# Input loads, one-hot moves and the gate's weights issued at other places of an attention and mixture-of-experts kernel

## The chip, the core and the metric

The kernel runs on one core of a Trainium2 chip. The metric is the device time of one execution in microseconds (us). Lower is better. The core has a matrix engine (PE, with its weight loads shown as PEld), two elementwise engines (DVE and ACT), a third, slower elementwise engine (POOL), and a queue engine (SP) that issues nearly all data transfers of this kernel, one after the other in program order. Each engine works through its own list of instructions in order. A transfer is done by the core's 16 DMA engines after SP has issued it.

## The reference

Three stages follow each other. The first is attention in which a query sees only the keys of its own hash bucket; the second is a dense mixture of eight experts with balanced gates; the third gives each token to one expert.

```python
# attention: q, k, v are (2, 8, 768, 64), proj is (64, 6)
q_bits = (einsum('bhsd,dk->bhsk', q, proj) > 0)      # and k_bits alike
mask = q_bucket[:, :, :, None] == k_bucket[:, :, None, :]
scores = where(mask, scale * q @ k.T, -1e9)
attn = exp(scores - max); attn = attn / (sum(attn) + 1e-9)
x = attn @ v                                         # then (1536, 512)
# experts, dense: w_gate (512, 8), w1 (8, 512, 1024), w2 (8, 1024, 512)
P = exp(x @ w_gate - max)
for _ in range(8): P /= P.sum(1) ; P /= P.sum(0) ; P *= N / E
x = sum over e of P[:, e] * (relu(x @ w1[e]) @ w2[e])
# experts, one per token: greedy by sorted logits, at most N / E tokens each
out[mask_e] = relu(x[mask_e] @ w1b[e]) @ w2b[e]
```

## The kernel before, in words

**Attention.** The 16 heads are taken as eight pairs (`n` = 0 to 7). A pair has two heads of 768 queries, so twelve tiles of 128 queries (`TU = 12`); the text calls the tiles of a pair r0 to r11. One pass of the loop `for t in range(NT + ...)` (L400) writes the instructions of tile `t` and of older tiles that are at later steps. The order is fixed by hand: `PLANS` (L25) lists, for even and odd tiles, which step comes when and how many tiles it lags, and a manual schedule keeps that order on every engine. The steps are:

- `qk` (L277): four PE products into the scores `S`. The operands are the stacked tiles `qa`, `ka`, `qb`, `kb`: rows 0 to 63 hold q or k in a high and a low part, rows 64 to 127 of `qb` and `kb` hold one-hot codes of the bits, so that the mask falls out of the same products.
- `soft`, `expo`, `inv`, `norm`: the maximum on DVE (L284), the exponential on ACT (L289), the reciprocal on DVE (L296), and the multiplication on POOL (L301), three tiles behind.
- `tr` (L309): PE transposes the normalised tile `e`, four to six tiles behind; ACT and DVE split it into two parts (L317, L321); `av` (L331) multiplies with v.
- `xa` and `xp`: after the second head's `av`, ACT copies the sums out (L351) to tiles called `x`, `idle` and `pz` in turn, SP moves them to the other half of the partitions (L352, L353: `xm`, `xc`), and POOL adds and splits them into `X`, the input of the experts (L363 to L365). This happens in tiles r2 to r8 of the next pair: the three pairs of transfers are `xm<-x`, `xm<-idle`, `xm<-pz`, each with its `xc`.
- `pp`, `pa`, `pd` in tiles r0 to r9: the next pair is prepared. PE transposes its q in r0 and r1 and its k in r2 and r3 (L170), ACT and DVE split them (L177 to L182), the bits follow in r4 and r5 (L199), the one-hot tiles `hot0` and `hot1` in r6 to r9 (L222, L230). Finished parts are put on a list, `MOVES`, and SP issues what was on the list at a tile's start at that tile's end (`move`, L159): six moves for q, six for k, two for each `hot`.
- `pv` (`ahead_v`, L372): POOL splits v (L254, L257), and `load(n + 2)` fetches q, k and v of the pair after the next with six transfers (L82).

The tiles `rq`, `rk`, `rv` have two buffers each, so the load of pair n + 2 waits until those of pair n have been read. For pair 0 the last read of `rv` is the step of `PREP_V` at tile 8.

```python
PREP_V = (3, 3, 6, 8)
...
        if r == TU - 1 and n + 2 < NP:
            load(n + 2)
...
        due = len(MOVES)
        for nm, lag, *part in PLANS[t % 2]:
...
        if due:
            move(due)
```

**Experts.** Behind the loop the order is a scheduler's. The weights come in 512 KB pieces through three `raw` buffers and are split into a high part (ACT, L431) and a low part (DVE, L432) in `big`. The gate's products (24 matmuls, L480 and L481, with the weights `wgs` that DVE makes from `wgr`, L466 to L469) give the gate `P`; eight rounds of balancing on DVE, with one small PE product each (L509), run beside the hidden products of the first expert (L567), which is followed by its output products (L586).

Of the kernel before, what the change touches and what calls it, by code (L numbers as in the profile page):

```python
# [9 lines left out]
F32 = mybir.dt.float32  # L10
F32R = mybir.dt.float32r
# [4 lines left out]
OP = mybir.AluOpType  # L16
# [22 lines left out]
def rd(x):  # L39
    return x.bitcast(F32)  # L40
# [3 lines left out]
def kernel(ctx, tc, q, k, v, proj, wg1, w1, w2, wg2, w1b, w2b, out):  # L44
    nc = tc.nc
# [3 lines left out]
    E = wg1.shape[1]  # L49
    F = w1.shape[2]  # L50
    R = S // 128
    NP = B * H // 2
    HP = H // 2
# [4 lines left out]
    consts = ctx.enter_context(tc.tile_pool(name="consts", bufs=1))  # L58
# [10 lines left out]
    ap = actx.enter_context(tc.tile_pool(name="attn", bufs=1))  # L69
# [4 lines left out]
    def load(n, what="qkv"):  # L74
        b, hp = divmod(n, HP)
        for nm, src in (("q", q), ("k", k), ("v", v)):
            if nm in what:
                t = ap.tile([128, R, 2, D], F32, name="r" + nm, bufs=2)
                rows = (slice(0, R // 2), slice(R // 2, R)) if n == 0 and nm != "v" else (slice(0, R),)
                for rs in rows:  # L80
                    for s in range(2):
                        nc.sync.dma_start(t[:, rs, s, :], src[b, 2 * hp + s].rearrange("(p r) d -> p r d", r=R)[:, rs])  # L82
                RAW["r" + nm, n] = t
# [13 lines left out]
    nc.gpsimd.memset(zero, 0.0)  # L97
    pid = ap.tile([128, NB], I32, name="pid")
    nc.gpsimd.iota(pid, pattern=[[0, NB]], base=0, channel_multiplier=1)
    pj = ap.tile([128, 256], F32, name="pj")  # L100
    nc.gpsimd.memset(pj, 0.0)
    pz = ap.tile([128, 256], F32, name="pz")
    nc.gpsimd.memset(pz, 0.0)
# [41 lines left out]
    def stack(n, s, moves):  # L145

        if n == 0 and s == 1 and HELD is not None:
            HELD.append((n, s, moves))
            return
        MOVES.extend((dst[at:at + 64, s], src[64 * s:64 * s + 64]) for dst, at, src in moves)  # L150
        if n == 0:
            move()
# [3 lines left out]
    def move(n=None):  # L156

        for dst, src in MOVES[:n]:
            nc.sync.dma_start(rd(dst), rd(src))  # L159
        del MOVES[:n]  # L160
# [46 lines left out]
    def hot_rows(dst, t, w, s, on_dve=False):  # L207

        rows = slice(64 * s, 64 * s + 64)
        if on_dve:  # L210
            nc.vector.tensor_scalar(dst, t[rows], 0.5 * NB if w else 0.5 * (NB - 2), 1.0 if w else BIG,
                                    op0=OP.is_ge if w else OP.is_gt, op1=OP.subtract if w else OP.mult)
        else:
            nc.scalar.activation(dst, t[rows], AF.Sign if w else AF.Relu, bias=cb[rows, w:w + 1], scale=1.0 if w else BIG)

    def prep_hot(n, w, ch, part):
        c0, c1 = PC[ch]
        if part == 0:
            if ch == 0 and n:
                PREP["o", w, n] = ap.tile([128, S], F32R, name=f"hot{w}", bufs=1)  # L220
            t = (Sp[1] if n == 0 and w == ch == 1 else aps.tile([128, 512], F32, name="tp", bufs=3))[:, :c1 - c0]
            nc.tensor.matmul(t, pat[:, w], PREP["b", n][:, c0:c1], start=True, stop=True)  # L222
            PREP["t"] = t
        if part == 1 and n == 0:
            for s in range(2):
                hots0[s].append((ST[0][2 + w][64:128, s, c0:c1], PREP["t"], w, s))
            hot_rows(*hots0[0].pop(), on_dve=w != ch)
        elif part == 1:
            hot = PREP["o", w, n]
            nc.scalar.activation(hot[:, c0:c1], PREP["t"], AF.Sign if w else AF.Relu, bias=cb[:, w:w + 1],  # L230
                                 scale=1.0 if w else BIG)
            if ch == 1:
                dst = ST[n % 2][2 + w]
                for s in range(2):
                    stack(n, s, ((dst, 64, hot),))

    def prep(n, i, part):
        if i < 4:
            prep_t(n, "qk"[i // 2], i % 2, part)
        elif i < 6:  # L240
            prep_bits(n, i - 4, part)
        else:
            prep_hot(n, (i - 6) // 2, i % 2, part)
# [3 lines left out]
    def prep_v(n, i):  # L247
        x = RAW["rv", n]
        if i == 0:
            VS[n] = ap.tile([128, R, 2, 2, D], F32R, name="vv", bufs=2)  # L250
        vv = VS[n]
        s = i // 2
        if i % 2 == 0:
            nc.gpsimd.tensor_tensor(vv[:, :, s, 0, :], x[:, :, s, :],  # L254
                                    zero[:, :, None].to_broadcast([128, R, D]), op=OP.add)
        else:
            nc.gpsimd.tensor_tensor(vv[:, :, s, 1, :], x[:, :, s, :], rd(vv[:, :, s, 0, :]), op=OP.subtract)  # L257
# [4 lines left out]
    TU = 4 * U  # L262
# [109 lines left out]
    def ahead_v(t):  # L372
        n, r = divmod(t, TU)
        for i in range(4):
            if t == PREP_V[i]:
                prep_v(0, i)
        if r in (8, 10) and n + 1 < NP:
            prep_v(n + 1, r // 2 - 4)
        if r in (0, 2) and 0 < n < NP:
            prep_v(n, r // 2 + 2)  # L380
        if r == TU - 1 and n + 2 < NP:
            load(n + 2)

    STEPS = dict(qk=qk, soft=soft, expo=expo, inv=inv, norm=norm, tr=tr, th=trh, tl=trl, av=av, xa=xa, xp=xp, pp=lambda t: ahead(t, 0), pa=lambda t: ahead(t, 1), pd=lambda t: ahead(t, 2),
                 pv=ahead_v)
    patterns()
    for i in (0, 1, 2, 3, 4, 5, 6, 8, 7, 9):
# [9 lines left out]
        stack(*x)  # L397
    load(0, "v")
    load(1, "v")
    for t in range(NT + max(x[1] for x in PLANS[0])):  # L400
        due = len(MOVES)
        for nm, lag, *part in PLANS[t % 2]:
            if 0 <= t - lag < NT:
                STEPS[nm](t - lag, *part)
        if due:
            move(due)
# [6 lines left out]
    core = ctx.enter_context(tc.tile_pool(name="core", bufs=1, reuse_waits="tile"))  # L413
# [4 lines left out]
    def small_ps():  # L418
        return ps.tile([128, 512], F32, name="sp", bufs=2)
# [42 lines left out]
    ones = core.tile([128, 128], F32, name="ones")  # L462
    nc.gpsimd.memset(ones, 1.0)

    wgr = core.tile([128, HP, E], F32, name="wgr")
    nc.sync.dma_start(wgr, wg1.rearrange("(a p) e -> p a e", p=128))  # L466
    wgs = core.tile([128, HP, 2 * E], F32R, name="wgs")
    nc.vector.tensor_copy(wgs[:, :, :E], wgr)
    nc.vector.tensor_tensor(wgs[:, :, E:], wgr, rd(wgs[:, :, :E]), op=OP.subtract)  # L469
    acc = core.tile([128, C, Dm], F32, name="acc")  # L470

    def rows_to_cols(stat, movs, dst):
# [24 lines left out]
    t = small_ps()  # L497
# [276 lines left out]
    for blk in range(NX):  # L774
        Hs.append((as_h(bigx() if blk else big()), as_h(big())))
        if blk == NX - 1:
# [5 lines left out]
            hot = hotp[:, :C * HC // 2].bitcast(F16).rearrange("p (c n) -> p c n", c=C)  # L782
# [434 lines left out]
```

## Time and profile before

| | |
|---|---|
| median of three runs | 1594.1 us (1592.13 to 1594.23) |
| the profiled execution | 1593.44 us |
| its span, first to last instruction | 1591.7 us |
| granted TensorE clock, mean of the span | 0.994 |
| PE busy | 1548.0 us, 97% of the span |
| DVE, ACT, POOL busy | 809.2, 453.2, 269.9 us |
| attention | about the first 270 us |

The busy share is an average: in the experts PE hardly waits; in attention each of PE, DVE, ACT and POOL is busy for most of the time, and who waits for whom is read tile by tile. Times in rows are us from the start of the span. In a timeline row the first number is the start, the second the length, and a bracket says how long the engine sat idle before and what ended that.

### The profile page before, as it was taken

The page shows a single profiled execution, that of the slowest core. Times are in us where ns is not written, and L with a number is a line of the kernel's source. Part 1 is how long each engine was busy: PE and PEld are TensorE (multiplying, and loading weights), DVE is VectorE, ACT ScalarE, POOL GpSimd, SP SyncE. Part 2 cuts the span into 40 slices and gives each one's busy share as a digit, 9 for nine tenths or more (in the row PEclk, how much of TensorE's full clock was granted, in tenths as well). Part 3 has the DMA queues.
Part 4 walks back from the last instruction along what each step waited for, and adds up shares of the span by engine and source line. Part 5 has one row for each costly group of instructions (what it writes and reads, how often), then busy time and mean ns, then how long its engine had stood idle before and what let it go on. Part 6 is the DMA issues. An engine that isn't in the chain of part 4 may idle for free.

```text
span 1591.7 us, 21428 instructions
## 1 busy us (share of the span) xinstructions
PE 1548.0 (97%) x8482; PEld 1311.2 (82%) x8482; DVE 809.2 (51%) x1833; ACT 453.2 (28%) x855; POOL 269.9 (17%) x313
## 2 busy tenths in 40 slices
PE   7999998999999999999999999999999999999998
PEld 6888886788888888888888888888887767788998
DVE  6888886712433334333333332134676377567533
ACT  6787886211211211221221021021121210011343
POOL 4888887020000000000000000000000000111221
PEclk9999999999999999999999999999999999899999
DMA  8766662220200110120020020011000116545531
GB/s 190 167 146 164 147 138 66 67 93 0 93 14 14 66 40 1 53 67 1 27 93 1 14 80 27 0 54 53 1 14 14 40 40 224 180 180 183 195 136 31
DMA packets 89301, 123.84 MB, mean 78 GB/s; under 512 B 44336, under 2 KB 52016, under 8 KB 89200
## 3 DMA queue, kind: packets, MB, share of 16 engines
q1 hardware_dynamic: 81680, 109.88, 23.7%
q0 software_dynamic: 2176, 6.29, 1.3%
q10 hardware_dynamic: 5344, 6.30, 1.1%
q8 instruction: 67, 1.10, 0.3%
q14 instruction: 34, 0.28, 0.1%
HBM read 83.91 MB, written 9.44 MB: 59 GB/s over the span
## 4 chain that ended last, share of the span: by engine, by line
PE 85%; DMA 4%; ACT 3%; DVE 2%; SPq 2%; POOL 2%; issue 1%; POOLq 0%; ACTq 0%; DVEq 0%
PE hp L567 32%; PE yp L586 29%; PE hp L944 5%; PE yp L888 4%; PE yp L997 3%; PE S L277 2%; PE O L331 2%; PE tp L309 2%; PE yp L1000 1%; PE sp L1081 1%; ACT e L289 1%; DMA rq<-in_q_dram 1%; SPq L159 1%; PE tp L199 1%; DMA raw<-in_moe_w_dram 1%
## 5 line engine op out<-in xcount | busy, mean ns | idle before, releaser
L567 PE MATMUL hp<-X,big 128*128 128x512 f32 x2304 | 528.9, 390 | 0.0
L567 PEld LDWEIGHTS hp<-X,big 128*128 128x128 f32 x2304 | 431.7, 188 | 89.9
L586 PE MATMUL yp<-big 128*128 128x512 f32 x2016 | 461.2, 389 | 0.0
L586 PEld LDWEIGHTS yp<-big 128*128 128x128 f32 x2016 | 378.2, 188 | 78.4
L568 ACT ACTIVATE big<-hp 128x512 fp32r<-128x512 f32 x176 | 105.2, 598 | 755.9 <-PE hp L567 755.9
L569 DVE SCALAR_TENSOR_TENSOR big<-hp,big 128x512 fp32r<-128x512 f32 x176 | 121.6, 691 | 252.3 <-ACT big L568 252.3
L591 DVE SCALAR_TENSOR_TENSOR acc<-yp,P,acc 128x512 f32<-128x512 f32 x72 | 54.1, 751 | 258.4 <-PE yp L586 258.4
L869 POOL DMA_INDIRECT raw<-x2h,who x4 | 4.1, 1025 | 949.5 <-DVE wg2b L1066 939.1
L301 POOL TENSOR_TENSOR e<-e,w 128x768 f32<-128x768 f32 x96 | 138.9, 1468 | 42.7 <-DVE w L296 27.5
L321 DVE TENSOR_TENSOR al<-tp,ah 128x512 fp32r<-128x512 f32 x144 | 98.2, 683 | 15.8 <-ACT ah L317 13.3
L284 DVE TENSOR_REDUCE w<-S 128x1 f32<-128x768 f32 x96 | 91.3, 951 | 14.8 <-PE S L277 13.4
L944 PE MATMUL hp<-raw,big 128*128 128x192 f32 x488 | 93.7, 338 | 1.2 <-ACT raw L922 1.2
L317 ACT ACTIVATE ah<-tp 128x512 fp32r<-128x512 f32 x144 | 86.2, 600 | 25.2 <-PE tp L309 22.2
L289 ACT ACTIVATE e<-S,w 128x768 f32<-128x768 f32 x96 | 87.0, 906 | 2.0 <-DVE w L284 1.9
L309 PE MATMUL tp<-ident,e 128*128 128x128 f32 x576 | 84.6, 274 | 2.2 <-POOL e L301 2.1
L432 DVE TENSOR_TENSOR big<-raw,big 128x1024 fp32r<-128x1024 f32 x63 | 76.6, 1222 | 14.1 <-ACT big L431 14.0
L944 PEld LDWEIGHTS hp<-raw,big 128*128 128x128 f32 x488 | 79.7, 193 | 2.8 <-ACT raw L922 1.7
L431 ACT ACTIVATE big<-raw 128x1024 fp32r<-128x1024 f32 x63 | 64.9, 1054 | 34.1 <-DMA raw<-in_moe_w_dram 32.8
L331 PE MATMUL O<-ah,vv 128*128 128x256 f32 x288 | 72.9, 283 | 1.3 <-ACT xm L346 0.8
L331 PE MATMUL O<-al,vv 128*128 128x256 f32 x288 | 72.9, 282 | 0.0
L309 PEld LDWEIGHTS tp<-ident,e 128*128 128x128 f32 x576 | 66.5, 141 | 4.8 <-POOL e L301 3.7
L542 DVE SCALAR_TENSOR_TENSOR junk<-acc,wg2b 128x512 bf16<-128x512 f32 x96 | 66.0, 687 | 1.9
(257 smaller groups left out, 1578.3 us busy)
## 6 DMA issues: line engine op xcount, KB each, us to landing
raw<-in_moe_w_dram SPq DMA_DIRECT2D x67, 512.0 KB, 3.4
big<-in_moe_w_dram SPq DMA_DIRECT2D x32, 1024.0 KB, 7.5
qa<-qhi SPq DMA_DIRECT2D x32, 192.0 KB, 3.8
qb<-qlo SPq DMA_DIRECT2D x16, 192.0 KB, 4.1
ka<-khi SPq DMA_DIRECT2D x16, 192.0 KB, 4.3
ka<-klo SPq DMA_DIRECT2D x16, 192.0 KB, 4.0
kb<-khi SPq DMA_DIRECT2D x16, 192.0 KB, 4.3
rv<-in_v_dram SPq DMA_DIRECT2D x16, 192.0 KB, 4.3
```

The lines of the kernel that those rows point to most:

```text
L284: nc.vector.tensor_reduce(EN[t][:, 0, i:i + 1], Sp[i], op=OP.max, axis=AX.X, negate=True)
L289: nc.scalar.activation(e, Sp[i], AF.Exp, bias=w[:, 0, i:i + 1], scale=1.0, accum_out=w[:, 1, i:i + 1])
L301: nc.gpsimd.tensor_tensor(e, e, w[:, 3, i:i + 1].to_broadcast([128, S]), op=OP.mult)
L309: nc.tensor.transpose(p[:, y * 128:y * 128 + 128], EN[t + i][:, kt * 128:kt * 128 + 128], ident)
L317: nc.scalar.activation(ah, TP[t, x], AF.Copy)
L321: nc.vector.tensor_tensor(al, TP[t, x], rd(ah), op=OP.subtract)
L331: nc.tensor.matmul(o, VS[n][:, kt, s].rearrange("p a d -> p (a d)"), a[:, :, kt], start=(kt == 0 and a is ah), stop=(kt == R - 1 and a is al))
L567: nc.tensor.matmul(t, a, b, start=(i == 0), stop=(i == len(prods) - 1))
L568: nc.scalar.activation(hh[:, f], t, AF.Relu)
L569: nc.vector.scalar_tensor_tensor(hl[:, f], t, 0.0, rd(hh[:, f]), op0=OP.max, op1=OP.subtract)
L586: nc.tensor.matmul(t, a, b, start=(i == 0), stop=(i == len(prods) - 1))
L944: nc.tensor.matmul(opened[f], w[:, d, f * 128:f * 128 + 128], xt[:, d], start=(d == 0), stop=(d == HP - 1))
```

## The change

There are four edits and a change of buffer. The load of pair n + 2 is issued in tile r3 of pair n and no longer in r11. The two moves of a finished one-hot tile are issued by SP in the tile in which they are made (r7 and r9), and no longer through the list at the end of the next one. The gate's weights `wgr` are loaded at the start of the loop, and DVE splits them at tile 12; both stood behind the loop. To make room, the tile `pj` takes the buffer of `x1`, which is used later.

```diff
-    pj = ap.tile([128, 256], F32, name="pj")
+    pj = ap.tile([128, 256], F32, name="x1")
...
                 for s in range(2):
-                    stack(n, s, ((dst, 64, hot),))
+                    nc.sync.dma_start(rd(dst[64:128, s]), rd(hot[64 * s:64 * s + 64]))
...
-        if r == TU - 1 and n + 2 < NP:
+        if r == 3 and n + 2 < NP:
             load(n + 2)
...
+    wgr = consts.tile([128, HP, E], F32, name="wgr")
+    nc.sync.dma_start(wgr, wg1.rearrange("(a p) e -> p a e", p=128))
+    wgs = consts.tile([128, HP, 2 * E], F32R, name="wgs")
     for t in range(NT + max(x[1] for x in PLANS[0])):
+        if t == TU:
+            nc.vector.tensor_copy(wgs[:, :, :E], wgr)
+            nc.vector.tensor_tensor(wgs[:, :, E:], wgr, rd(wgs[:, :, :E]), op=OP.subtract)
...
-    wgr = core.tile([128, HP, E], F32, name="wgr")
-    nc.sync.dma_start(wgr, wg1.rearrange("(a p) e -> p a e", p=128))
-    wgs = core.tile([128, HP, 2 * E], F32R, name="wgs")
-    nc.vector.tensor_copy(wgs[:, :, :E], wgr)
-    nc.vector.tensor_tensor(wgs[:, :, E:], wgr, rd(wgs[:, :, :E]), op=OP.subtract)
```

On SP's list of pair 1, from the q moves (tile r2) to the third of the `xm`, `xc` pairs (r6), stood before:

```order
L159 DMA qb_121<-qlo 64x768
L352 DMA xm<-idle 64x256
L353 DMA xc<-idle 64x256
L159 DMA ka_120<-khi 64x768
L159 DMA ka_120<-klo 64x768
L159 DMA kb_122<-khi 64x768
L159 DMA ka_120<-khi 64x768
L159 DMA ka_120<-klo 64x768
L159 DMA kb_122<-khi 64x768
L352 DMA xm<-pz 64x256
```

and stands now:

```order
L159 DMA qb_121<-qlo 64x768
L82 DMA rq<-in_q_dram 128x6x64 x2
L82 DMA rk<-in_k_dram 128x6x64 x2
L82 DMA rv<-in_v_dram 128x6x64 x2
L352 DMA xm<-idle 64x256
L353 DMA xc<-idle 64x256
L159 DMA ka_120<-khi 64x768
L159 DMA ka_120<-klo 64x768
L159 DMA kb_122<-khi 64x768
L159 DMA ka_120<-khi 64x768
L159 DMA ka_120<-klo 64x768
L159 DMA kb_122<-khi 64x768
```

The six loads came in ahead of two of the three `xm`, `xc` pairs and of the k moves. Before, they stood behind the second one-hot's moves at the end of the pair. Pairs 2 to 5 read alike; pairs 6 and 7 have no loads.

In pair 0, SP's list from the last q move on was:

```order
L159 DMA qb_117<-qlo 64x768
L159 DMA ka_116<-khi 64x768
L159 DMA ka_116<-klo 64x768
L159 DMA kb_118<-khi 64x768
L159 DMA ka_116<-khi 64x768
L159 DMA ka_116<-klo 64x768
L159 DMA kb_118<-khi 64x768
L347 DMA xc<-xm 64x256
L159 DMA qb_117<-hot_380 64x768 x2
L347 DMA xc<-xm 64x256
L159 DMA kb_118<-hot_448 64x768 x2
```

and from the last of the loads on it is now:

```order
L82 DMA rv<-in_v_dram 128x6x64 x2
L159 DMA ka_116<-khi 64x768
L159 DMA ka_116<-klo 64x768
L159 DMA kb_118<-khi 64x768
L159 DMA ka_116<-khi 64x768
L159 DMA ka_116<-klo 64x768
L159 DMA kb_118<-khi 64x768
L235 DMA qb_117<-hot_392 64x768 x2
L347 DMA xc<-xm 64x256
L235 DMA kb_118<-hot_462 64x768 x2
```

The `rv` row waits for POOL's last read of pair 0's `rv`, in tile 8, because it takes over that buffer, and the k moves and one-hot moves for pair 1 now stand behind this wait.

On PE, behind the last gate product (`wgs`), the order of the small products (`acc`, `sm`, `P`) and the hidden products (`hp`) of the first expert was, before:

```order
L567 MATMUL hp<-X,big 128x512
L486 MATMUL sp<-ident,acc 128x16 x8
L567 MATMUL hp<-X,big 128x512 x2
L486 MATMUL sp<-ident,acc 128x16 x4
L567 MATMUL hp<-X,big 128x512 x9
L498 MATMUL sp<-ident,sm 128x128
L567 MATMUL hp<-X,big 128x512 x22
L509 MATMUL sp<-P,ones 128x96
L567 MATMUL hp<-X,big 128x512 x17
```

and is now:

```order
L487 MATMUL sp<-ident,acc 128x16 x12
L568 MATMUL hp<-X,big 128x512
L499 MATMUL sp<-ident,sm 128x128
L568 MATMUL hp<-X,big 128x512 x17
L510 MATMUL sp<-P,ones 128x96
L568 MATMUL hp<-X,big 128x512 x22
L510 MATMUL sp<-P,ones 128x96
L568 MATMUL hp<-X,big 128x512 x28
```

The twelve transposes of the gate's result now stand together ahead of the hidden products, and the first product of the balancing comes after 18 hidden products instead of 34. (Behind the loop the changed file's line numbers are one higher.)

## Rows read from the trace of the kernel before

**Rows 1.** Who waited for whom: PE, 0 to 272 us (total, times, longest).

```profile
PE S L277 <- DMA kb<-hot: 5.3, 6, 1.2
PE tp L170 <- DMA rq<-in_q_dram: 4.8, 4, 1.7
```

**Rows 2.** Timeline, PE: first products of tiles, and pair 4's first transposes.

```profile
45.63 0.60 PE L277 MATMUL S<-ka,qa 128*128 128x512 f32 x2
...
136.03 0.59 PE L277 MATMUL S<-ka,qa 128*128 128x512 f32 x2
...
141.04 0.52 PE L170 MATMUL tp<-ident,rq 128*128 128x128 f32 x3 [1.70 <-DMA rq<-in_q_dram]
141.31 0.60 PE L277 MATMUL S<-ka,qa 128*128 128x512 f32 x2
...
143.92 0.59 PE L277 MATMUL S<-ka,qa 128*128 128x512 f32 x2
...
146.10 0.59 PE L277 MATMUL S<-ka,qa 128*128 128x512 f32 x2
...
168.49 0.60 PE L277 MATMUL S<-ka,qa 128*128 128x512 f32 x2
...
204.59 0.60 PE L277 MATMUL S<-ka,qa 128*128 128x512 f32 x2
```

**Rows 3.** Timeline, SP (issue of transfers), pair 4 and the start of pair 5.

```profile
152.63 0.90 SPq L353 DMA_DIRECT2D xc<-idle  x1
...
159.25 0.94 SPq L353 DMA_DIRECT2D xc<-pz  x1
...
168.20 1.35 SPq L82 DMA_DIRECT2D rq<-in_q_dram  x2
...
173.02 0.58 SPq L347 DMA_DIRECT2D xc<-xm  x1
```

**Rows 4.** Timeline, POOL, pair 4, tiles r6 to r10.

```profile
156.05 0.74 POOL L363 TENSOR_TENSOR xm<-xm,xc 128x256 f32<-128x256 f32 x1 [0.97 <-DMA xc<-idle]
...
158.34 2.89 POOL L301 TENSOR_TENSOR e<-e,w 128x768 f32<-128x768 f32 x2
...
162.07 0.74 POOL L363 TENSOR_TENSOR xm<-xm,xc 128x256 f32<-128x256 f32 x1
...
164.27 2.89 POOL L301 TENSOR_TENSOR e<-e,w 128x768 f32<-128x768 f32 x2
```

**Rows 5.** Timeline, PE: the second transposes of pair 4's tiles r8 and r10.

```profile
160.98 0.60 PE L309 MATMUL tp<-ident,e 128*128 128x128 f32 x4
...
165.79 0.66 PE L309 MATMUL tp<-ident,e 128*128 128x128 f32 x4
```

**Rows 6.** Windows: busy time by engine, PEclk, DMA share and GB/s of three stretches.

```profile
147.00:160.00 13.00, 13.00 (x99) 12.56 (x98) 11.32 (x21) 10.34 (x23) 11.53 (x12) 1.00 0.84 196
169.00:175.00 6.00, 4.21 (x32) 3.81 (x32) 4.39 (x8) 3.77 (x8) 5.18 (x5) 1.00 1.12 230
...
274.00:278.00 4.00, 4.00 (x12) 1.36 (x11) 1.06 (x1) 1.83 (x2) 1.09 (x3) 0.57 0.92 334
```

**Rows 7.** Timeline, POOL, SP and PE, end of pair 0 and start of pair 1.

```profile
34.26 1.02 POOL L257 TENSOR_TENSOR vv<-rv,vv 128x384 fp32r<-128x384 f32 x1
...
39.72 1.24 SPq L159 DMA_DIRECT2D kb<-hot  x2
...
42.74 0.59 PE L277 MATMUL S<-kb,qb 128*128 128x512 f32 x2 [1.17 <-DMA kb<-hot]
```

**Rows 8.** Timeline, SP, PE and POOL, end of attention and first expert.

```profile
271.14 0.59 SPq L466 DMA_DIRECT2D wgr<-in_moe_w_gate_dram  x1
...
273.80 0.40 PE L480 MATMUL sp<-X,wgs 128*16 128x512 f32 x1 [4.29 <-DVE wgs L469]
...
274.29 0.73 POOL L365 TENSOR_TENSOR X<-xm,X 128x256 fp32r<-128x256 f32 x1
...
285.50 5.28 PE L567 MATMUL hp<-X,big 128*128 128x512 f32 x22
```

## The prediction

> **What bounds the kernel now.** I read the busy shares first: PE works in nearly all of the span, and in the experts it hardly waits, so a change outside them can only move the first 300 us. For those I took PE's waits [rows 1]. The two largest are both at the start of a pair: the first tile's score products wait for the second one-hot tile's move, and the transposes of the next pair's q wait for its load. Then I went through PE tile by tile. In pair 4 the first tile r0 takes from 136.03 to 141.31, 5.28 us, of which 1.70 are a wait for `rq`; a tile with the same PE work, r2, takes from 143.92 to 146.10, 2.18 us [rows 2]. The rest, r1 to r11, takes 27.18 us (141.31 to 168.49), and from pair 1 to pair 6 the second tiles start 31.79 us apart (45.63 to 204.59, five pairs). So an average r0 takes 31.79 - 27.18 = 4.61 us, and 2.43 us of it are waiting. That is what earlier loads and one-hots can win in a pair.
>
> In r1 to r11 PE runs nearly without holes, but not with much room. POOL multiplies the tiles that PE then transposes, and in the same list it waits for the transfers `xc`. In pair 4 it stands idle for 0.97 us until `xc<-idle` has landed, at 156.05; the product for tile r4 then ends at 158.34 + 2.89/2 = 159.79 [rows 4], and PE's transposes of it start at 160.98 [rows 5]: 1.19 us of slack. In r10 there is none: POOL's product for r6 ends at 164.27 + 1.45 = 165.72, and PE starts on it at 165.79. So whatever delays POOL after tile r6 delays the pair's end.
>
> **The change, part by part.** *Stalls removed.* With the loads eight tiles and the one-hot moves one tile earlier, both waits of r0 end before PE comes to them: -2.43 us in each of the pairs 2 to 6 (pair 1 below). In pair 7 nothing is prepared, and only the wait for the one-hots falls, 5.3/6 = 0.9 us [rows 1].
>
> *Loads moved past others.* SP issues in order, and the six loads now stand ahead of `xm<-idle`, `xc<-idle`, the six k moves, `xm<-pz` and `xc<-pz`. In the trace SP works through this stretch without a pause (`xc<-idle` at 152.63, `xc<-pz` at 159.25, [rows 3]), so all of it comes later by what the loads take; call it D. On POOL, `xc<-idle` already lands last. By the order of its list, the products for r4, r5, the third addition and the products for r6 and r7 all stand behind that wait. POOL's row at 156.05 becomes 156.05 + D, PE's transposes in r8 wait D - 1.19, those in r10 are D late in all, and the pair ends D later. What is late next (the one-hot moves, the next pair's r0) moves along with PE and costs no more.
>
> D is bounded by rows. At the start of pair 5 the six loads keep SP from 168.20 to 173.02, 4.82 us [rows 3]. Below: issued into an empty queue, a transfer of that size takes SP 1.24/2 = 0.62 us [rows 7], so 3.7 us. Above: six loads are 1.18 MB, and the DMA engines are as good as full in both stretches, with 196 GB/s among the moves and 230 among the loads [rows 6]; that is 6.0 or 5.1 us. I take 5.0, near the loads' own rows. The k moves that are also pushed back have until the next r0, some 15 us, and are hidden.
>
> The page "DMA: Bandwidth & Descriptors" of the Trainium skill, section "Why small descriptors are slow (HBM only)", says that pieces of 256 bytes from HBM lose 27% to overhead, while transfers inside SBUF don't. The loads' pieces have 64 floats, so by that rule a load would take longer than a move of the same size; an estimate from it is 1.27 x 6.0 = 7.6 us for D, which would put the kernel at 1618. The rows show the loads no slower than the moves, 230 against 196 GB/s, and decide.
>
> So each of five pairs (r1 of pair 1 to r1 of pair 6) changes by 5.0 - 2.43 = +2.57 us: **+12.9**.
>
> *Pair 0.* Its `rv` load waits for POOL's read that ends at 34.26 + 1.02 = 35.28 [rows 7]. Behind it stand two `rv` loads, six k moves, two moves of the first one-hot and a small `xc`; at 0.62 to 0.80 us each for the ten and 0.5 for the small one, `kb<-hot` is issued at 42.0 to 43.8 instead of 39.72, so pair 1's first scores, which go on at 42.74 with its landing, go on 2.3 to 4.1 us later. I take 3.3, since the DMA engines then have ten transfers at once. Pair 1's own wait for `rq` comes off: from 42.74 to the next tile at 45.63 [rows 2] are 2.89 us, where the work is that of r0, 2.18 us, less the half of the scores that is done before, some 0.35; so 1.1. Net **+2.2** (1.2 to 3.0).
>
> *Gate's weights.* In pair 0 the load of 16 KB costs SP one issue, 0.59 us [rows 8], and the two small DVE operations fall at tile 12, where PE waits anyway: nothing; without that cover, 1 us. Behind attention PE waits 4.29 us until `wgs` is there and starts at 273.80. Now the gate's products can start at once, and only the last two need the `X` that POOL has written by 274.29 + 0.73 = 275.02. But the hidden products behind them need the first expert's weights, whose first transfer starts only 0.6 us earlier, and the fourth piece of those waits for one of three buffers. Below: 0.6. Above: the whole wait and the slow clock behind it (0.57 granted in 274 to 278 [rows 6], so 4 x 0.43 = 1.7): 6.0. Between them: by 285.50 only 12 hidden products were through. In the 4.4 us from the end of the gate products (about 281.1) those needed 12 x 0.24 (5.28/22) = 2.9, so 1.5 us were holes; and where 12 products stood ahead of the small ones that wait on the balance, 18 that need only three pieces of the weights do now, 6 x 0.24 = 1.4 us. I take their sum, **-3**.
>
> The new buffer of `pj` costs nothing: it is read before tile 0, its second owner comes in pair 1.
>
> **Sum.** 12.9 + 2.2 - 0.9 - 3 = +11.2 us. The profiled execution took 1593.44 us, 0.7 less than the median of the runs, 1594.1; on the median, 1605.
>
> **Rivals.**
> *Faster: the loads vanish in the burst.* If SP or the DMA engines had room between the q and k moves that the rows don't show, POOL would not come later. D = 0 gives 1594.1 - 5 x 2.43 + 2.2 - 0.9 - 3 = 1580. It decides below D = 2.77, where the sum is zero. For it: the DMA share among the moves is 0.84, not 1. Against it: 0.16 of 13 us is 2.1 us of room at most, and SP itself needs 3.7 us for six issues.
>
> *No change: the loads run at the rate of large pieces.* In 274 to 278 the weights come in at 334 GB/s [rows 6]. At that rate D = 1.18 MB/334 = 3.5, so 5 x 1.07 + 2.2 - 0.9 - 3 = +3.7, or 1598, and with a somewhat larger gain at the end of attention within what can be told from no change. Against it stand 196 and 230 GB/s for pieces of this shape. The same page, "Specifications", gives 358 GB/s as a core's limit from HBM; that would make D 3.3 as an estimate, and no row shows it.
>
> *Slower still: the clock falls.* PE would stand still for about D - 1.19 = 3.8 us in r8 of five pairs. Behind the one pause of such length, 4.29 us, the granted clock was 0.57 for 4 us, the lower of the two levels (1.2 GHz) for most of them. Five times 1.7 us make +8.5, so 1614. Against it: PE waits again in r10, which hides most of that.
>
> **How the numbers follow.** Faster or slower by 0.2%, 3.2 us, is what a measurement of this kernel can tell from no change. Forecast, slower with D from 3.7 to 6.0: 0.75. Faster: 0.13. No change: 0.06. Slower still: 0.06. The forecast's ends are 5 x 1.27 + 1.2 - 0.9 - 5 = +1.7 and 5 x 3.57 + 3.0 - 0.9 - 0.6 = +19; with not all terms at one end at once, 1596 to 1613 leaves out the faster rival and little else. Of the forecast's 0.75, 0.06 lie within 0.2% and 0.01 below: faster 0.14, same 0.12, slower 0.74.
>
> **What would show it.** Right: PE has no wait for `rq` or `kb<-hot` from pair 2 on, and r0 takes about 2.2 us; POOL's wait for `xc<-idle` grows from 1 to about 6 us in pairs 1 to 5; PE waits for POOL's `e` in r8 and r10, some 5 us a pair; pair 1 starts some 2 us late, with SP waiting for POOL in pair 0; the gate's products start right behind attention. Wrong: if POOL's waits for `xc` stay near 1 us, the loads are free and the kernel is faster; if r0 keeps its length, its stall had another cause.

## The result, and the profile after

The changed kernel takes 1615.1 us (median of four runs, 1614.5 to 1620.1), the kernel before took 1593.1 on the same chip (1591.5 to 1594.2, four runs): 1.0146 times as long, with a 95% interval of 1.0123 to 1.0169. That is 22.0 us slower, in the direction and by the mechanism that was forecast, but twice as much as the forecast's 11.2, and just outside its range.

The profile is that of the longest of the four runs (1620.07 us, span 1618.1, mean granted clock 0.981), so its parts add up to more than 22. To see where the time lies I cut both traces at the same instructions: the second tile of pair 1, that of pair 6, the last product of attention and the first hidden product of the second expert. Two of these marks of before stand in [rows 2]; the other two are these rows of its PE timeline:

```profile
269.23 0.28 PE L331 MATMUL O<-al,vv 128*128 128x256 f32 x1
...
330.67 21.92 PE L567 MATMUL hp<-X,big 128*128 128x512 f32 x96
```

The same marks, and the places that the forecast spoke of, in the PE timeline of the changed kernel:

```profile
48.88 0.98 PE L277 MATMUL S<-kb,qb 128*128 128x512 f32 x2 [5.30 <-DMA kb<-hot]
...
52.28 0.99 PE L277 MATMUL S<-ka,qa 128*128 128x512 f32 x2
...
160.35 0.59 PE L277 MATMUL S<-ka,qa 128*128 128x512 f32 x2
...
178.52 0.59 PE L277 MATMUL S<-ka,qa 128*128 128x512 f32 x2
...
184.36 1.11 PE L309 MATMUL tp<-ident,e 128*128 128x128 f32 x4 [4.20 <-POOL e L301]
...
185.60 0.84 PE L277 MATMUL S<-ka,qa 128*128 128x512 f32 x2
...
188.77 0.60 PE L277 MATMUL S<-ka,qa 128*128 128x512 f32 x2
...
192.92 0.60 PE L277 MATMUL S<-ka,qa 128*128 128x512 f32 x2
195.10 0.59 PE L277 MATMUL S<-ka,qa 128*128 128x512 f32 x2
...
231.81 0.59 PE L277 MATMUL S<-ka,qa 128*128 128x512 f32 x2
...
297.12 0.28 PE L331 MATMUL O<-al,vv 128*128 128x256 f32 x1
297.24 0.39 PE L481 MATMUL sp<-X,wgs 128*16 128x512 f32 x1
...
356.48 21.92 PE L568 MATMUL hp<-X,big 128*128 128x512 f32 x96
```

The changed kernel was profiled once more among the experiments (label `again`). The two traces together, in us:

| stretch | before | after | change | change, `again` | forecast |
|---|---|---|---|---|---|
| start to r1 of pair 1 | 45.63 | 52.28 | +6.6 | +6.2 | +2.2 |
| r1 of pair 1 to r1 of pair 6 | 158.96 | 179.53 | +20.6 | +22.5 | +12.9 |
| from there to the last product of attention | 64.64 | 65.31 | +0.7 | -0.8 | -0.9 |
| to the second expert's first product | 61.44 | 59.36 | -2.1 | -2.9 | -3 |
| the rest | 1261.03 | 1261.62 | +0.6 | -3.3 | 0 |
| sum | | | +26.4 | +21.8 | +11.2 |

In the last line both kernels do the same; over all profiles of this study, whatever the kernel, it lies between 1257.8 and 1262.0. That is a difference between executions, not one that the change makes. The excess over the forecast lies mainly in the first two lines.

Who waited for whom, in the changed kernel (PE from 0 to 300 us, SP from 0 to 60, POOL from 0 to 300; total, times, longest):

```profile
PE tp L309 <- POOL e L301: 25.1, 9, 5.3
PE S L277 <- DMA kb<-hot: 5.3, 1, 5.3
...
SPq L82 <- POOL vv L257: 4.7, 1, 4.7
...
POOL xm L363 <- DMA xc<-idle: 34.3, 6, 7.4
```

Against [rows 1], the wait for `rq` is gone and that for the one-hots is left only once, at the start of pair 1. In their place stands a wait for POOL's products, in r8 of pairs 1 to 5, and behind POOL stands its own wait for `xc<-idle`: the chain that the forecast described. SP's list and POOL's in pair 4, from the six q moves on:

```profile
166.46 1.18 SPq L159 DMA_DIRECT2D qa<-qhi  x2
...
169.95 0.70 SPq L159 DMA_DIRECT2D qb<-qlo  x1
170.71 2.29 SPq L82 DMA_DIRECT2D rq<-in_q_dram  x2
173.04 1.75 SPq L82 DMA_DIRECT2D rk<-in_k_dram  x2
174.88 1.52 SPq L82 DMA_DIRECT2D rv<-in_v_dram  x2
176.50 0.91 SPq L352 DMA_DIRECT2D xm<-idle  x1
177.46 0.59 SPq L353 DMA_DIRECT2D xc<-idle  x1
```

```profile
180.67 0.72 POOL L363 TENSOR_TENSOR xm<-xm,xc 128x256 f32<-128x256 f32 x1 [6.36 <-DMA xc<-idle]
...
182.84 2.90 POOL L301 TENSOR_TENSOR e<-e,w 128x768 f32<-128x768 f32 x2
```

SP issues `xc<-idle` 17.11 us after r1 of the pair began (160.35), where it was 152.63 - 141.31 = 11.32 in [rows 2, 3]; POOL goes on 20.32 us after it, where it was 14.74 [rows 4]. PE stands still 4.20 us in r8 and starts r9 at 185.60, not 2.1 us after 178.52 but 7.1. What the windows say of the granted clock, at the start of pair 1 and around the wait of pair 4 (busy time of PE, PEld, DVE, ACT and POOL with the number of instructions, then PEclk, DMA share, GB/s):

```profile
47.00:52.00 5.00, 3.12 (x14) 3.05 (x15) 1.80 (x4) 0.39 (x1) 0.03 (x1) 0.54 0.41 89
...
184.00:188.00 4.00, 3.64 (x17) 3.45 (x18) 1.58 (x2) 1.95 (x4) 3.84 (x6) 0.59 0.70 179
188.00:192.00 4.00, 4.00 (x32) 3.81 (x31) 2.79 (x7) 3.57 (x8) 4.00 (x4) 1.00 0.33 87
```

Behind both waits PE runs for most of these 4 to 5 us at the lower level (1.2 GHz), and r9 takes 3.17 us (185.60 to 188.77) where it took 2.4. On first sight this looks like the rival "slower still". The next section settles whether it is.

### The profile page after: what moved, and what is told of

Read it like the earlier page. It is cut to its first block, busy times and chain, and to the rows that moved or that the text cites. A ratio compares the mean times of both kernels' runs of the same rounds, so it can differ in the third digit from the quotient of the medians.

```text
span 1618.1 us, 21457 instructions
## 1 busy us (share of the span) xinstructions
PE 1563.5 (97%) x8482; PEld 1327.6 (82%) x8482; DVE 809.0 (50%) x1833; ACT 452.6 (28%) x855; POOL 269.6 (17%) x313
## 4 chain that ended last, share of the span: by engine, by line
PE 89%; DVE 3%; DMA 3%; POOL 2%; issue 1%; ACT 1%; SPq 1%; POOLq 0%; DVEq 0%; ACTq 0%
PE hp L568 32%; PE yp L587 28%; PE hp L945 5%; PE yp L889 4%; PE S L277 3%; PE tp L309 3%; PE O L331 3%; PE yp L998 3%; PE yp L1001 1%; PE sp L1082 1%; DMA xc<-idle 1%; PE tp L199 1%; POOL e L301 1%; PE yp L1003 1%; PE tp L170 1%
## 5 line engine op out<-in xcount | busy, mean ns | idle before, releaser
L309 PE MATMUL tp<-ident,e 128*128 128x128 f32 x576 | 89.0, 283 | 25.1 <-POOL e L301 25.1
L309 PEld LDWEIGHTS tp<-ident,e 128*128 128x128 f32 x576 | 69.8, 146 | 28.1 <-POOL e L301 27.0
```

What stands on the lines that cost most here:

```text
L309: nc.tensor.transpose(p[:, y * 128:y * 128 + 128], EN[t + i][:, kt * 128:kt * 128 + 128], ident)
```

## The experiments

Twelve kernels, each timed against the kernel before on its own chip. The changed kernel itself stands first.

| label | what is different | median, us | ratio to before, 95% |
|---|---|---|---|
| `again` | nothing | 1616.0 | 1.0134 (1.0116 to 1.0153) |
| `fill` | PE kept busy in r8's wait | 1619.0 | 1.0143 (1.0126 to 1.0160) |
| `loads_only` | loads in r3, nothing else of the change | 1626.5 | 1.0200 (1.0185 to 1.0215) |
| `pair0_late` | pair 0's loads in r11 | 1610.0 | 1.0111 (1.0095 to 1.0128) |
| `loads_r9` | loads in r9 | 1607.1 | 1.0072 (1.0058 to 1.0086) |
| `xc_act` | xm, xc of j = 1, 2 issued by ACT | 1589.2 | 0.9965 (0.9952 to 0.9979) |
| `rq_r3` | rq alone in r3, the rest in r11 | 1589.1 | 0.9962 (0.9947 to 0.9977) |
| `spread` | rq in r7, rk in r8, rv in r10 | 1589.4 | 0.9974 (0.9963 to 0.9984) |
| `gate_only` | only the gate's weights early | 1591.0 | 0.9982 (0.9972 to 0.9993) |
| `loads_back` | all of the change but the loads' place | 1581.3 | 0.9933 (0.9919 to 0.9948) |
| `loads_r10` | loads in r10 | 1578.9 | 0.9910 (0.9896 to 0.9925) |
| `rq_r8` | rq in r8, rk and rv in r11 | 1578.2 | 0.9904 (0.9889 to 0.9918) |

Two theories of the excess stood against each other: A, the loads delay what stands behind them by more than forecast, and nothing else costs; B, the lower clock behind each wait costs as well.

**`again`.** The changed kernel without any edit.

> The changed kernel once more, as the control for the others on this chip. Every theory: 1613 to 1617 us. In its trace PE waits some 4 us for POOL's product in tile r8 of pairs 1 to 5. Theory A (the loads delay the transfers behind them on SP, and nothing else costs): r9 takes the 2.4 us of before, and the lost time of a pair is D alone. Theory B (late transfers, and behind each wait a lower granted clock): r9 takes 3 to 4.5 us, with the granted clock between 0.5 and 0.8 in the 4 us behind the wait.

In pairs 1 to 5, r9 takes 3.26 to 4.44 us, so the clock is low behind each wait, as B says. That a low clock costs anything is not shown by it yet.

**`fill`.** Products of constants take PE through the wait of r8:

```diff
         p = aps.tile([128, 512], F32, name="tp", bufs=3)
+        if x == 0 and t % TU == 4 and TU < t < 6 * TU:
+            for _ in range(28):
+                nc.tensor.matmul(p[:, :256], pat[:, 0], pat.rearrange("p a b -> p (a b)"), start=True, stop=True)
         for y in range(4):
```

> The changed kernel with 28 products of constants put into the transposes' PSUM tile just ahead of the transposes that wait in r8 of pairs 1 to 5 (results overwritten, about 3.4 us at the full clock, where the wait is some 4.2 us). PE so stands still for under 1 us there, while the transfers come as late as before. Theory A: nothing changes, 1613 to 1617 us. Theory B: the granted clock stays at 1.0 in r9, r9 takes 2.4 to 2.8 us; PE then waits for POOL's next product in r10 as forecast, so the pair's delay falls from 6.4 us to D, about 5.6 us: 5 x 0.8 = 4 us, 1608 to 1612 us. If r10 shows no wait either, r9's whole 1.45 us and the slow part of r8 come off: 1604 to 1608 us.

PE's timeline in pair 4 of this kernel, r8 to r10, and one row of its windows:

```profile
177.80 3.50 PE L309 MATMUL tp<-pat 128*128 128x256 f32 x28
183.38 0.65 PE L312 MATMUL tp<-ident,e 128*128 128x128 f32 x4 [2.08 <-POOL e L301]
...
184.05 0.52 PE L277 MATMUL S<-ka,qa 128*128 128x512 f32 x2
...
186.43 0.61 PE L277 MATMUL S<-ka,qa 128*128 128x512 f32 x2
...
189.21 0.66 PE L312 MATMUL tp<-ident,e 128*128 128x128 f32 x4 [1.11 <-POOL e L301]
189.62 0.60 PE L277 MATMUL S<-ka,qa 128*128 128x512 f32 x2
```

```profile
184.00:186.00 2.00, 2.00 (x17) 1.91 (x16) 1.24 (x2) 1.87 (x4) 2.00 (x3) 1.00 0.44 131
```

PE still waits 2.08 us, but the granted clock stays at 1.00 and r9 takes 2.38 us (184.05 to 186.43). Then it waits once more, 1.11 us in r10, for POOL's next product. In pairs 1 to 4 r9 takes 2.4 us; in pair 5, where PE waits 2.25 us behind the constants, the clock falls (0.69 from 219 to 223 us) and r9 takes 3.94. The five pairs take 35.87 us each from r1 to r1, 36.30 in `again` and 35.91 in the first profile; the time, 1619.0, lies above the ranges of both theories and is not shorter than that of `again` (the intervals overlap). So most of what the low clock takes is time in which PE would have waited for POOL anyway: A carries most of the excess.

The times alone don't make B nothing, though. In this trace POOL goes on after `xc<-idle` 21.32 us after r1 on average, where it is 20.88 and 20.93 in the two traces of the changed kernel, and that hides a gain. Counted from POOL's going on to the start of r11, pair 2 takes 11.39 us in the changed kernel, with r9 at 4.44, and 9.96 us here:

```profile
109.32 0.72 POOL L363 TENSOR_TENSOR xm<-xm,xc 128x256 f32<-128x256 f32 x1 [6.38 <-DMA xc<-idle]
...
120.71 0.60 PE L277 MATMUL S<-ka,qa 128*128 128x512 f32 x2
```

```profile
108.37 0.74 POOL L366 TENSOR_TENSOR xm<-xm,xc 128x256 f32<-128x256 f32 x1 [7.09 <-DMA xc<-idle]
...
118.33 0.60 PE L277 MATMUL S<-ka,qa 128*128 128x512 f32 x2
```

In pair 4 both take 9.95 us. Over pairs 1 to 5 it is 10.46 us on average in the first profile, 10.79 in `again` and 10.07 here: by these traces the low clock costs 0.4 to 0.7 us a pair, 2 to 4 us in all. No time shows that.

**`loads_only`.** The kernel before, with `if r == 3` in place of `if r == TU - 1` at the load.

> The kernel before with the loads alone moved to tile r3; one-hot moves and gate's weights as before. If the loads carry the loss (theories A and B): the boundary's gain of 2.1 us and some 0.9 us of one-hot wait a pair are missing, so 1617 to 1622 us, slower than the changed kernel. Rival (the one-hot moves that are issued at once, or the gate's load in pair 0, carry a good part of the loss): under 1610 us.

At 1626.5 it is slower than the changed kernel by 10.5 us, more than expected; PE's waits for `kb<-hot` come to 10.9 us over six here, 5.8 of them in pair 1. The other edits of the change are gains, and the loads' place costs all of the loss and more.

**`loads_back`.** The changed kernel with `if r == TU - 1` again at the load.

> The changed kernel with the loads back in tile r11: one-hot moves at once and the gate's weights early remain. If the loads' place alone is at fault: faster than before. The wait for the one-hots (some 0.9 us a pair) falls away, the loads are issued about 1.2 us earlier since the one-hot moves no longer stand just ahead of them, and PE comes to rq about 0.9 us earlier, so some 1.4 us of 1.7 stay of that wait: 6 x 1.2 + 0.9 + 2.1 = 10 us less than before, 1584 us (1580 to 1590). Rival (the one-hot moves issued at once collide with other transfers and cost as much as they save): 1590 to 1594 us, the boundary's gain alone.

1581.3 us, 12 less than before: a little better than expected. PE's long waits have none for `kb<-hot` any more, and r0 takes 2.9 to 4.3 us in pairs 2 to 6. The place of the loads alone thus costs some 34 us: `again` is 21.2 us slower than the kernel before on its own chip, this one 12.4 faster. One row of PE's waits here bears on an edit that the forecast costed at nothing:

```profile
PE tp L170 <- DVE wgs L406: 1.0, 1, 1.0
```

The split of the gate's weights holds up PE in r0 of pair 1 for 1.0 us, as the forecast had it for the case that the cover is gone; in the changed kernel the wait for `kb<-hot` covers it.

**`gate_only`.** The changed kernel without the other two edits.

> The kernel before with the gate's weights early (and the buffer of pj), loads and one-hot moves as before. By the traces the first expert's end moves 2.1 us nearer to the end of attention, and pair 0's start shows up to 1.5 us of loss: 1590 to 1593 us. By the forecast's 3 us: 1590 us.

2.7 us less than before, by the medians; from the last product of attention to the second expert's first it takes 58.2 us instead of 61.4.

**`pair0_late`.** The load with `if r == (TU - 1 if n == 0 else 3)`.

> The changed kernel with the loads of pair 0 alone back in tile r11, all others in r3. This prices pair 0's term. By its trace (second tile of pair 1 at 52.3 us where it was 45.6): SP has no wait for POOL in pair 0, kb<-hot is issued some 5 us earlier, and the second tile of pair 1 starts at 46 to 47 us with PE waiting for rq there; 1609 to 1611 us. By the forecast's price of 2.2 us for pair 0: 1613 us.

It is 16.3 us slower than the kernel before on its chip, where `again` is 21.2 us slower: 5.0 us less, with intervals that overlap (6.0 by the medians, which are of two chips). In the trace r1 of pair 1 starts at 43.90, 8 us earlier than in `again`, and 1.7 earlier than in the kernel before, which still waits for the one-hots there. The forecast's price of 2.2 us for pair 0 was too low.

**`rq_r3`.** A third of the loads in r3:

```diff
-        if r == 3 and n + 2 < NP:
-            load(n + 2)
+        if n + 2 < NP:
+            if n == 0 and r == TU - 1:
+                load(n + 2)
+            elif n and r in (3, TU - 1):
+                load(n + 2, "q" if r == 3 else "kv")
```

> The kernel with the loads back in r11, and rq alone moved to tile r3, ahead of xm<-idle and xc<-idle (pair 0 keeps all six in r11). It tests the forecast's sum with a smaller D. If a pair's end moves by what is issued ahead of xc<-idle (two loads, 1.35 to 2.3 us, and up to 0.5 us of later landing, so D about 2.2): POOL waits some 3 us for xc<-idle, PE in r8 about 1 and in r10 the rest; against 1581 us that is 5 x (2.2 - 1.0 of rq's wait in r0) = +6, 1587 us (1583 to 1591). If two loads find room where six don't: 1574 to 1579 us.

As expected of the sum. POOL's and PE's waits in this kernel:

```profile
POOL xm L363 <- DMA xc<-idle: 16.3, 6, 3.4
...
PE tp L309 <- POOL e L301: 11.7, 12, 1.2
```

PE waits about 1 us in r8 and as long again in r10, r9 takes 2.4 us, and a pair takes 31.63 us from r1 to r1. The same kernel with rq in r8 (below) takes 29.55, so two loads ahead of `xc<-idle` cost a pair 2.08 us, and six cost 35.9 - 29.55 = 6.4, three times as much. A load costs about 1 us, with no free room for a small number of them.

**`xc_act`.** On top of `pair0_late`, ACT issues the second and third pair of xm and xc:

```diff
-            nc.sync.dma_start(xm[D:], x1[:D])
-            nc.sync.dma_start(xc[D:], x1[D:])
+            dma = nc.scalar if j and n < 7 else nc.sync
+            dma.dma_start(xm[D:], x1[:D])
+            dma.dma_start(xc[D:], x1[D:])
```

> The changed kernel with pair 0's loads in r11, and with xm<-idle, xc<-idle, xm<-pz and xc<-pz issued from ACT's queue right behind the copy that feeds them, so that the six loads of r3 are no longer ahead of them in any queue but share the DMA engines with them. If D is SP's order: POOL waits under 2 us for xc<-idle, no wait in r8, r0 2.2 us: 1610 - 5 x 6 = 1580 us, up to 1588 if the four issues (0.5 to 0.9 us each) hold ACT up. If D is the room on the DMA engines: the transfers land as late as before, 1605 to 1612 us.

ACT's timeline in pair 4 of this kernel, and two rows of POOL's waits:

```profile
151.24 0.49 ACTq L353 DMA_DIRECT2D xm<-idle  x1
151.82 1.04 ACTq L354 DMA_DIRECT2D xc<-idle  x1
```

```profile
POOL xm L364 <- DMA xc<-idle: 6.7, 7, 1.6
POOL xm L364 <- DMA xc<-pz: 5.7, 4, 2.8
```

POOL's wait falls to about 1 us each, r8 has none, and some 21 us come back against `pair0_late`; the time is 1 us above what was expected, and r5 and r7 are 0.5 and about 1 us longer in each pair, probably because ACT spends time on the issues, 1.5 us on these two. So D is the place in SP's list. How much of it is SP's time and how much the engines' backlog this run does not tell, since ACT issues `xc<-idle` before SP comes to the loads; `xc<-pz`, which ACT issues as SP ends with them, lands up to 2.8 us late.

**`loads_r9`.** The load with `if r == 9`.

> The changed kernel with the loads issued in tile r9 and not in r3, so behind the k moves and behind all three pairs of xm and xc. Theories A and B: no wait in r8, and r0 keeps its 2.2 us, so five pairs win 2.25 us each (r0 of 4.52 us on average before, 2.27 after), pair 0 about 1, pair 7 0.9, the boundary 2.1: 1593 - 15 = 1578 us, range 1575 to 1584. Rival (the loads then hold up the second one-hot's moves and the xc transfers behind them, and PE waits for kb<-hot at the start of a pair again): 1 to 3 us a pair come back, 1584 to 1593 us.

A miss: 1607 us, worse than the rival too. SP's and PE's timelines around the start of pair 5 show why:

```profile
175.02 1.34 SPq L82 DMA_DIRECT2D rq<-in_q_dram  x2
...
179.82 1.26 SPq L235 DMA_DIRECT2D kb<-hot  x2
```

```profile
181.31 0.59 PE L277 MATMUL S<-ka,qa 128*128 128x512 f32 x2
184.87 0.96 PE L277 MATMUL S<-kb,qb 128*128 128x512 f32 x2 [2.97 <-DMA kb<-hot]
```

Within r9 the load's step comes before the one that issues the second one-hot, so its six transfers stand ahead of `kb<-hot`. The wait left r8 and came back at the next pair's start, as rival but larger: r0 takes 5.2 to 7.7 us in pairs 2 to 6.

**`spread`.** `load(n + 2, "q")` in r7, `"k"` in r8, `"v"` in r10.

> The changed kernel with the six loads in three pieces where SP has gaps: rq in tile r7 (behind the last xm and xc), rk in r8, rv in r10 behind the second one-hot's moves. Theory (only what stands ahead of xm, xc and the one-hots hurts): no wait in r8 and none in r0, so five pairs win 2.25 us each, pair 0 about 1, pair 7 0.9, the boundary 2.1: 1593 - 15 = 1578 us (1575 to 1583). Rival (as with the loads in r9, kb<-hot lands late behind whatever is issued ahead of it: two loads, about 1.8 us): 1 to 2 us a pair come back, 1584 to 1590 us.

1589.4, the rival's upper end. PE waits four times for `kb<-hot`, 6.5 us in all, once for 4.0: it stands behind rk, and in pair 3, where the wait is 4.0, it lands 6.9 us after its issue, with rv issued right behind it. That rv is what delays it is not shown. And r1 of pair 1 starts at 48.32, later than before.

**`loads_r10`, `rq_r8`.** The load with `if r == 10`; and rq alone in r8, behind the first one-hot (as the diff of `rq_r3`, with 8 for 3).

> The changed kernel with the six loads in tile r10: right behind the second one-hot's moves and ahead of one xc<-xm that waits for a copy on ACT. They are issued up to 0.8 us earlier than with r11 (SP idle between kb<-hot and xc<-xm there), so up to 0.8 of rq's wait a pair is won: 1577 to 1581 us. Rival (what stands behind the loads, xc<-xm and the next pair's moves, becomes late): 1582 to 1588 us.

> The kernel with the loads back in r11, and rq alone moved on to tile r8, behind the first one-hot's moves, where SP has nothing to issue for some 2 us and two loads take 1.3 (pair 0 keeps all six in r11). If the rest of r0's excess is rq's late landing (r0 takes 3.2 to 4.3 us in pairs 2 to 6 of that kernel, 2.2 without a wait): about 1 us a pair, 1581 - 5 = 1576 us (1573 to 1579). Rival (the second one-hot's moves land later behind rq, as they did when rq and rk were spread over r7 and r8): no gain or a loss, 1581 to 1588 us.

Both come out as expected, 1578.9 and 1578.2 us, and both beat the kernel before and the changed one by far more than their intervals. They can't be told from each other. SP's timeline of `rq_r8` in pair 4:

```profile
152.46 1.18 SPq L235 DMA_DIRECT2D qb<-hot  x2
153.68 1.34 SPq L82 DMA_DIRECT2D rq<-in_q_dram  x2
155.13 0.58 SPq L347 DMA_DIRECT2D xc<-xm  x1
156.87 1.15 SPq L235 DMA_DIRECT2D kb<-hot  x2
```

SP is idle from 155.71 to 156.87 even with rq there: the load takes only time that was free, and r0 takes 2.18 us in each of the pairs 2 to 6.

## Why the prediction was right or wrong

**The direction and the chain were right.** The loads stand ahead of `xc<-idle`, POOL waits for it, PE for POOL in r8, and the end of the pair moves by D. `loads_back` takes away the loads' place, `xc_act` takes xm and xc from behind it, and the loss goes: both are faster than the kernel before, `xc_act` by less.

**The stalls removed: nearly right.** r0 took 4.52 us on average in pairs 2 to 6 and takes 2.27: 2.25 won, of 2.43 forecast. r1 got 0.31 longer (2.92 on average, 2.61 before).

**D was mis-sized: this is the step that failed.** "I take 5.0, near the loads' own rows", with 6.0 as the upper end. Over pairs 1 to 5 POOL goes on 20.88 us after r1 instead of 14.54: D = 6.34. SP issues `xc<-idle` 5.50 us later (16.90 after r1, 11.40 before), and it then takes 3.98 us until POOL goes on, instead of 3.14. The first part is half a microsecond above the forecast: the loads of [rows 3] had only two one-hot moves right ahead of them, while behind the six q moves the six loads hold SP for 5.24 us on average (the two of `rq` alone 1.6 to 2.1 us there in `rq_r3`, 1.3 to 1.4 in r8 in `rq_r8`). The second part, 0.84, has no term in the forecast at all: D was counted to the issue, but POOL waits for the landing. Over the five profiles with the six loads ahead of `xc<-idle` on SP this part is 0.28 (`pair0_late`) to 1.31 (`fill`); why it varies is open. From r8 to r10 five pairs so lose 6.1 us each, 2.25 come off, 0.3 come on in r1: about 4.1 x 5 = 20.6, instead of 2.57 x 5. In `again` it is 4.5 a pair.

The forecast weighed a rule on this and set it aside. The Trainium skill's page "DMA: Bandwidth & Descriptors", section "Why small descriptors are slow (HBM only)", counts 3 of the 11 cycles of a 256-byte piece from HBM as overhead, 27%, and says that transfers between SBUF tiles don't suffer it. The runs don't bear it out here. Behind the six q moves the loads do hold SP longer than those moves, 5.24 against 4.26 us on average. But in `rq_r8`, with less ahead of them, the six loads take 4.0 us of SP in four of five pairs, and the six q moves 4.2. And in pair 4 of the changed kernel 222 GB/s are moved while the loads are issued (170.7 to 176.4 us) and 174 during the q moves (166.4 to 170.7). So the longer hold goes with what stands ahead of the loads. The forecast's estimate by the rule, 7.6, was also worked out wrongly: 3 of 11 cycles make 11/8 of 6.0, 8.25 as an estimate.

**"PE waits again in r10, which hides most of that": right.** The clock fell, as the rival had it, and r9 became 1.4 us longer on average, but by the traces it cost 0.4 to 0.7 us a pair and not the 1.7 of the rival (`fill`). The forecast had no term for that part. The rival named a time near the result (1614), mostly by luck: the larger part of the excess is D's.

**Pair 0 was mis-sized: the second term that failed.** 6.6 us instead of 2.2 (`again`: 6.2). In the first profile 7.7 us of the excess over the forecast are the five pairs', 4.4 are pair 0's. POOL's last read of `rv` ended at 36.86, not at 35.28 as in [rows 7], and so did SP's wait (in `again` `rv` is issued at 35.66); from there the ten transfers and a small one took until 45.36:

```profile
36.89 1.24 SPq L82 DMA_DIRECT2D rv<-in_v_dram  x2
...
45.36 1.19 SPq L235 DMA_DIRECT2D kb<-hot  x2
```

That is 8.47 us, the top of what the forecast's 0.62 to 0.80 each allow. So PE goes on at 48.88, 6.1 us later than in [rows 7]. From there to r1 the forecast counted 1.8 us; it took 3.40, at a granted clock of 0.54. No wait for POOL stands behind that one to hide it, so this clock probably did cost; no run here kept PE busy there.

**The gate's weights: right in size.** The forecast was 3 us, `again` shows 2.9, the first profile 2.1, and the kernel with that edit alone is 2.7 us faster. The two parts of the forecast's sum (holes filled, products moved ahead) were not measured apart.

**The rival "faster"** (the loads vanish in the burst) was refuted for the loads, but its time of 1580 is that of the change with its loads elsewhere.

## What to carry to other kernels

Before moving a transfer to an earlier place in an in-order issue queue, list what it is moved ahead of and ask who waits for that: here two loads cost a pair 2.1 us and six 6.4, about 1 us each, and the free places were the gaps in which the queue had nothing to issue (`rq_r8`). Size such a delay up to the landing, not to the issue, and from a row with the same traffic ahead of it. A lower clock behind a wait is not a loss in full: keep the engine busy through the wait and see how much of the time the next wait takes instead. Where the total can't tell, measure from the event that releases the chain (here POOL's going on) to the end of the stretch.

## What the runs showed of the hardware that was not expected

Six loads that hold SP for 4.5 to 5.0 us behind two moves hold it for 4.8 to 5.7 behind six, and a small transfer issued behind them takes 0.84 us longer until its reader goes on (0.28 to 1.31 over five profiles of kernels with the loads there). Issuing two small transfers from ACT took 1.5 us of ACT's time in pair 4, as much as on SP. With 3.5 us of products put into PE's wait of pair 4 the granted clock stayed at 1.00, although PE stood still for another 2.08 us; in pair 5, behind the same products and 2.25 us of standing still, it was 0.69 from 219 to 223 us; in the changed kernel, after 4.20 us without work, it was 0.59 over the next 4 us.
